# A windowed attention and gated feed-forward kernel: unit 1's attention in the wide band form, a new order of work, three aligned places in TensorE's code

## The chip, the core and the metric

The kernel runs on one core of a Trainium2 chip. The core has TensorE (matrix products), VectorE, ScalarE and GpSimd (elementwise work), SyncE (which issues the DMAs here), an on-chip memory, and eight banks of PSUM into which TensorE writes. The metric is the device time of one execution, in microseconds.

In the profile's rows PE is TensorE's matmuls and PEld its weight loads, DVE is VectorE, ACT ScalarE, POOL GpSimd, SP SyncE.

## The reference

Attention over 8 batches and 8 heads, 576 positions of 64 values, in which a position sees itself and the 63 before it; then a feed-forward stage with token shift and a gate. Everything is float32.

```
scores = (q @ k.T) / sqrt(64)
mask   = (rel >= 0) & (rel < 64)          # rel = pos[:, None] - pos[None, :]
attn   = softmax(where(mask, scores, -1e9))
x      = (attn @ v), heads side by side   # 8 x 576 x 512
xk = mu_k * x + (1 - mu_k) * x_prev       # x_prev: one position back
xr = mu_r * x + (1 - mu_r) * x_prev
k  = relu(xk @ w_k)                       # 512 -> 1024
out = sigmoid(xr @ w_r) * ((k * k) @ w_v)
```

The weights and `v`, `q`, `k` come as the reference gives them; the weights arrive as 64-bit words and are decoded on the chip.

## The kernel before

**Units and groups.** The 8 x 576 positions are cut into nine units of 512 positions. A unit has four groups, one for each pair of heads (128 of the 512 columns), so there are 36 groups `g`; two neighbouring groups make a pair `j = g // 2`. For each unit the attention of its four groups gives `xT`, `mix` turns that into the operands `xs` (or `xm` in unit 0) of the products, and `r_units`, `k_units` and `v_units` do the three products with 512 columns each.

**Three forms of attention.** The first four groups (unit 0, `WHOLES`) work on blocks of 128 x 128 and transpose on TensorE. Groups 4 to 7 (unit 1, below `WIDE`) have four bands of 32 partitions, each with four blocks of 32 queries of one group: per group 32 score calls and 48 value calls. From group 8 on (`g >= WIDE`) a pair of groups shares its bands: two bands a group, each with eight blocks of queries, half of the score work of both groups in each of the two calls, so that a score call needs the queries and keys of both groups; the values need 40 calls a group. A call in float32 stands in the machine's code as two weight loads and two matmuls, so a pair's values are 192 matmuls below `WIDE` and 160 from it on, and its scores 128 in either form. The softmax between them runs as `least` and `exp` (VectorE, ScalarE), `shares` (sums and reciprocals), `scale` (GpSimd or VectorE) and `turn`, VectorE's transposition, one for each group and half (lines 778 to 853).

**The stage before the products.** In unit 0 the weights are decoded: each of 20 parts (4 of `w_r`, 8 of `w_k`, 8 of `w_v`) passes `sign` (ScalarE), `clamp`, `shift`, `top`, `low` (VectorE, some clamps on GpSimd), `first_part` and `second_part` (lines 405 to 455). Unit 0's r and k products use `low`'s output straight, as `whole`, in float32; everything else uses the two halves, `ws`, three matmuls to a product of 128 x 512.

**What sets the order.** Every step is a `Piece` with the engines it may run on, a cost, what it needs and which buffers it takes (`room`: 8 banks, 2 `qk` buffers, 3 `v` buffers, and so on). `play()` lays the pieces out on a modelled clock; `p.fn(p.engine)` then emits them in that order, and each engine runs its instructions in the order emitted. `ORDER` (line 86) fixes by number what each engine plays first, which covers unit 0, unit 1 and the beginning of unit 2; after that `play()` chooses by key and by the modelled clock, in which TensorE's costs come from `clocked`. `Hold` counts the uses of a buffer.

**What the steps below touch.** `values` (line 643) writes the value calls; at the first group of a pair it can call `addr_align` (line 650), which places the next instruction of TensorE's code at a given slot; up to `max_nops` slots are filled with idle instructions, and more are jumped over. With `PLACED = 18` no pair is ever placed, since `j` ends at 17. `load_v` (line 559) loads the value blocks, six of 32 rows to a band and group below `WIDE`, five from it on. `first_mask` (line 368) writes the two masks for bands with a batch's first queries.

Of the kernel before, what the change touches and what calls it, by code (L numbers as in the profile page):

```python
# [33 lines left out]
NC, NF = DM // P, DF // P  # L34
# [15 lines left out]
WHOLE = 859  # L50
# [12 lines left out]
WIDE = 8  # L63
# [14 lines left out]
ALIGN, SKIP = 102, 12  # L78
PLACED = 18
# [5 lines left out]

ORDER = {
# [10 lines left out]
    ),  # L97
    "DVE": (
# [12 lines left out]
    ),  # L111
    "ACT": (
# [11 lines left out]
    ),  # L124
    "POOL": (
# [4 lines left out]
    ),  # L130
# [17 lines left out]
def attn_rwkv_kernel(ctx, tc, qT, kT, v2, mu_k, mu_r, w_k, w_v, w_r, out):  # L148
# [49 lines left out]
    def play():  # L198

        left, free, now, begun, port, bus, landed, run = {}, {}, 0, [], 0, 0, [], None  # L200
        moved, clock = 0, [WINDOW, 0, True]
# [5 lines left out]
        def clocked(t, work):  # L207
            ratio = 2.37 if work == 440 else 1.92
            tick(t)
            while True:  # L210
                r = ratio if clock[2] else 1
                if t + work * r <= clock[0]:
                    clock[1] += work * r
                    return t + work * r
                clock[1] += clock[0] - t
                work, t = work - (clock[0] - t) / r, clock[0]
                tick(t)
# [19 lines left out]
        while any(left.values()) or any(script.values()):  # L237
# [8 lines left out]
            for e, ps in left.items():  # L246
# [3 lines left out]
                for _, n, p in ([(0, 0, given[-1])] if given else ps):  # L250
# [29 lines left out]
                    if e == "PE":  # L280
                        free[e] = p.done = clocked(now, p.costs[e])
                    else:
                        free[e] = p.done = now + p.costs[e]
# [359 lines left out]
    def values(g):  # L643

        j, n = divmod(g, 2)
        if n == 0:
            flipped[j] = [bank(2 * P) if g >= WIDE else bank(2, P) for _ in bands]

            if j >= PLACED:
                tc.keep_in_program_order(nc.tensor.addr_align(128, offset=ALIGN, max_nops=SKIP))  # L650
# [65 lines left out]
    def run_x(keys, j):  # L716
# [35 lines left out]
        for n, g in enumerate(pair):  # L752
            needs = every[n] if whole else sum(every, [])
            uses = [*held["v", g], *(chain.pop((g, h, "pt")) for h in range(2))]
            if whole:
                for half in range(2) if g in HALVES else (None,):
                    one = [Hold("bank"), Hold("x"), Hold("x")]
                    part = 1 if half is None else 2
                    p = Piece("PE", keys[n], 1100 / part, lambda e, g=g, half=half: whole_values(g, half),
# [5 lines left out]
            p = Piece("PE", keys[0], (1091 if ps else 1340) - 170 * (g >= WIDE), lambda e, g=g: values(g), [*needs, *ps], [x for o in own for x in o], uses)  # L765
# [322 lines left out]
    def begin(k):  # L1088
        return BEGIN[k] if k < len(BEGIN) else 10 * k - 60
# [10 lines left out]
    for g in range(PAIRED):  # L1100
        if g >= NC:
            load_qk(g, key=begin(g - 1) - 1)
            load_v(g, key=begin(g) - 1)
        if g == WHOLES:
            built = Piece("POOL", begin(g) - 8, 3300, band_mask, port=True)
            built = chain["masks"] = Piece("POOL", begin(g) - 4, 900, lambda e: first_mask(e, 0), [built, chain["least"]], port=True)
        run_s(begin(g), g, 1000 if g < WHOLES else 870)
        if g < WHOLES:
            for h in range(2):
                turn_whole(begin(g) + 1, g, h)  # L1110
        if g % 2:
            run_x((begin(g - 1) + 2, begin(g) + 2), g // 2)
    for j in range(PAIRED // 2, len(groups) // 2):
# [3 lines left out]
        if 2 * j % NC == 0 and u in (2, 4):  # L1117
            built = chain["masks"] = Piece("POOL", pair_at(j) - 4, 1200, lambda e, b=u // 4: first_mask(e, b, b + 2),
                                           [built, *chain.pop("firsts")], port=True)
        before = None  # L1120
        for g in (2 * j, 2 * j + 1):
            p = run_s(pair_at(j), g, 970 if before else 870)
# [67 lines left out]
```

## Time and profile before

| | us |
|---|---|
| median of three runs (613.45 to 615.07) | 614.35 |
| the profiled execution's own time | 613.81 |
| its span, first to last instruction | 612.0 |
| TensorE busy | 596.7 |
| VectorE busy | 395.0 |
| ScalarE busy | 371.0 |
| GpSimd busy | 141.9 |

All rows come from the one profiled execution, whose span is 1.81 us shorter than its time. TensorE is busy in every fortieth of the span to nine tenths or more but the first and the last. A matmul's row is its start, its length with a modelled end, and how many follow each other on the same tiles; the distance between the starts of two rows is what TensorE spent on the first.

### The profile page before, as it was taken

To read this page: it belongs to the slowest core of one execution; us is meant where nothing else is said; L and a number is where in the kernel's file an instruction comes from. 1 tells how busy PE (TensorE), PEld (TensorE's weight loads), DVE (VectorE), ACT (ScalarE), POOL (GpSimd) and SP (SyncE) were. 2 spreads that over 40 slices of the span, in tenths; PEclk is the share of its full clock that TensorE was granted. 3 is DMA by queue.
4 is the path that set the end of the run, shared out by engine and by line. 5 is a ranking of instruction groups with operands and counts; after the bars stand their busy time and mean duration, and the time that the engine had idled before them with its cause. 6 is when DMAs were issued, how large, how long until landed. Compare 5 with 4: busy or idle time off the path is not lost.

```text
span 612.0 us, 17692 instructions
## 1 busy us (share of the span) xinstructions
PE 596.7 (98%) x7072; PEld 465.6 (76%) x7072; DVE 395.0 (65%) x1208; ACT 371.0 (61%) x1060; POOL 141.9 (23%) x208
## 2 busy tenths in 40 slices
PE   4999999999999999999999999999999999999997
PEld 3654577878888888888888888877888888888885
DVE  4899999909783667556763677276827583665211
ACT  5988967448476736683577358644766466734630
POOL 6575557502300230011201130023002300201000
PEclk9999999999999999999999999999999999999999
DMA  8997122213431223122312222132212230010001
GB/s 252 337 331 224 54 86 81 70 51 83 132 93 43 76 73 116 29 75 71 101 42 59 91 77 74 44 109 80 76 44 93 74 97 24 2 54 17 1 18 52
DMA packets 57426, 53.59 MB, mean 88 GB/s; under 512 B 10496, under 2 KB 50944, under 8 KB 57344
## 3 DMA queue, kind: packets, MB, share of 16 engines
q1 hardware_dynamic: 57344, 52.46, 28.1%
q8 instruction: 56, 0.92, 0.6%
q14 instruction: 26, 0.21, 0.1%
HBM read 43.00 MB, written 9.44 MB: 86 GB/s over the span
## 4 chain that ended last, share of the span: by engine, by line
PE 88%; DMA 7%; ACT 2%; DVE 1%; SPq 1%; issue 1%; ACTq 0%
PE bank L166 88%; DMA raw<-w_v 3%; DMA v<-v 2%; SPq L166 1%; DMA raw<-w_k 1%; DMA qk<-kT 1%; ACT pr L166 1%; DVE bank L166 1%; ACT kf L166 1%; DVE r L166 0%; ACT ws L166 0%; ACT wt L166 0%; DVE rs L166 0%; ACT ks L166 0%; DVE whole L166 0%
## 5 line engine op out<-in xcount | busy, mean ns | idle before, releaser
L166 PE MATMUL bank<-xs,ws 128*128 128x512 f32 x1152 | 273.2, 396 | 0.0
L166 PEld LDWEIGHTS bank<-xs,ws 128*128 128x128 f32 x1152 | 215.8, 188 | 50.9
L166 PE MATMUL bank<-ks,ws 128*128 128x512 f32 x864 | 206.7, 397 | 1.4 <-issue 1.4
L166 PEld LDWEIGHTS bank<-ks,ws 128*128 128x128 f32 x864 | 161.0, 188 | 40.2 <-issue 1.5
L166 DVE TENSOR_TENSOR ks<-kf,ks 128x512 fp32r<-128x512 f32 x69 | 51.1, 746 | 112.9 <-ACT ks L166 112.9
L166 ACT ACTIVATE pr<-pr,nmax 128x96 f32<-128x96 f32 (+1 forms) x288 | 105.0, 366 | 11.7 <-DVE nmax L166 11.1
L166 ACT ACTIVATE kf<-bank 128x512 f32<-128x512 f32 x72 | 43.0, 597 | 67.3 <-PE bank L166 65.4
L166 POOL CAST ks<-kf 128x512 fp32r<-128x512 f32 x8 | 4.9, 611 | 256.0 <-ACT kf L166 256.0
L166 DVE CUSTOM_DVE_ANT_0 pr<-bank,bands 128x96 f32<-128x96 f32 x256 | 49.4, 249 | 13.4 <-PE bank L166 13.2
L166 ACT COPY xT<-bank 128x256 f32<-128x256 f32 (+1 forms) x46 | 15.7, 391 | 65.1 <-PE bank L166 64.9
L166 ACT ACTIVATION_READ_ACCUMULATOR pr<-pr,nmax 128x1 f32 x288 | 54.1, 188 | 0.0
L166 ACT ACTIVATE kf<-kf 128x512 f32<-128x512 f32 x71 | 44.7, 631 | 1.9
L166 DVE SCALAR_TENSOR_TENSOR r<-bank,r 128x512 f32<-128x512 f32 x36 | 24.5, 680 | 32.3 <-PE bank L166 32.3
L166 PE MATMUL bank<-xm,whole 128*128 128x512 f32 x96 | 43.8, 601 | 1.0 <-DVE whole L166 1.0
L166 ACT ACTIVATE th<-bank 128x512 f32<-128x512 f32 x36 | 21.3, 591 | 35.8 <-PE bank L166 24.6
L166 PEld LDWEIGHTS bank<-pt,v 32*64 32x64 f32 (+1 forms) x2720 | 35.7, 131 | 9.4 <-issue 7.1
L166 ACT CAST ks<-kf 128x512 fp32r<-128x512 f32 x64 | 39.5, 619 | 1.7
L166 PE MATMUL bank<-qk 64*32 64x96 f32 (+1 forms) x2112 | 33.4, 254 | 7.3 <-DMA qk<-qT 5.9
L166 PEld LDWEIGHTS bank<-qk 64*32 64x32 f32 (+1 forms) x2112 | 28.2, 108 | 15.3 <-issue 12.5
L166 PE MATMUL bank<-pt,v 32*64 32x96 f32 (+3 forms) x2720 | 38.6, 243 | 0.3 <-ACT kf L166 0.3
L166 DVE TENSOR_TENSOR xs<-d,xs 128x512 fp32r<-128x512 f32 x59 | 37.9, 685 | 0.0
L166 ACT CAST xs<-d 128x512 fp32r<-128x512 f32 x49 | 28.8, 617 | 14.2 <-POOL d L166 12.7
(79 smaller groups left out, 547.4 us busy)
## 6 DMA issues: line engine op xcount, KB each, us to landing
v<-v SPq DMA_DIRECT2D x76, 64.0 KB, 2.1
raw<-w_k SPq DMA_DIRECT2D x8, 512.0 KB, 7.2
raw<-w_v SPq DMA_DIRECT2D x8, 512.0 KB, 5.6
v<-v SPq DMA_DIRECT2D x52, 48.0 KB, 2.0
v<-v SPq DMA_DIRECT2D x68, 32.0 KB, 2.0
raw<-w_r SPq DMA_DIRECT2D x4, 512.0 KB, 6.0
outT<-r SPq DMA_DIRECT2D x8, 256.0 KB, 2.1
qk<-kT SPq DMA_DIRECT2D x8, 224.0 KB, 4.2
```

The costliest lines, as they stand in the source:

```text
L166: return lambda *args, **kw: tc.keep_in_program_order(op(*args, **kw))
```

## The change

`WIDE` goes from 8 to 4, so unit 1's groups 4 to 7 take the form of the later units: `values`, `scores`, `load_v`, `run_s`, `run_x` and `soften` follow by their conditions on `g`. Their queries, keys and values are loaded two groups at a time, and the masks for a batch's first queries are made once for units 1 to 3 (bands 0 and 2) and once more at unit 4, where before they were made for unit 1, for unit 2 and for unit 4.

`addr_align` is now called for pairs 3, 6 and 11, with slots 228, 59 and 56 of 256, before the pair's values.

`play()` has two costs more, `ENTER` and `LEAVE`, when TensorE goes from full to tiled matmuls and back, and other costs for the tiled pieces. The tables in `ORDER` are new and shorter; the rest of the order follows `play()` as before.

```
-WIDE = 8
+WIDE = 4
...
-ALIGN, SKIP = 102, 12
-PLACED = 18
+PLACES, SKIP = {3: 228, 6: 59, 11: 56}, 12
...
+ENTER, LEAVE = 95, 281
...
 ORDER = {
     "PE": (
-        509, 510, 535, 531, 566, 533, 559, 557, 561, 555, 590, 563, 1503, 1510, 1517, 586, 1524, 588, 633, 1518,
+        509, 510, 535, 531, 566, 533, 559, 561, 557, 555, 590, 563, 1502, 1509, 1516, 1523, 588, 586, 645, 614,
...
-        def clocked(t, work):
-            ratio = 2.37 if work == 440 else 1.92
+        def clocked(t, work, ratio):
...
                     if e == "PE":
-                        free[e] = p.done = clocked(now, p.costs[e])
+                        work, at = p.costs[e], now
+                        before, tiled = tiled, work not in (440, 697, WHOLE)
+                        if before is not None and tiled != before:
+                            at = clocked(at, ENTER if tiled else LEAVE, 1)
+                        free[e] = p.done = clocked(at, work, 1.8 if tiled else 2.37 if work == 440 else 1.92)
...
-            if j >= PLACED:
-                tc.keep_in_program_order(nc.tensor.addr_align(128, offset=ALIGN, max_nops=SKIP))
+            if j in PLACES:
+                tc.keep_in_program_order(nc.tensor.addr_align(256, offset=PLACES[j], max_nops=SKIP))
...
-            p = Piece("PE", keys[0], (1091 if ps else 1340) - 170 * (g >= WIDE), lambda e, g=g: values(g), [*needs, *ps], [x for o in own for x in o], uses)
+            p = Piece("PE", keys[0], 908 if g >= WIDE else 1074, lambda e, g=g: values(g), [*needs, *ps], [x for o in own for x in o], uses)
...
-        if g >= NC:
-            load_qk(g, key=begin(g - 1) - 1)
-            load_v(g, key=begin(g) - 1)
+        for x in range(g, g + 2) if g >= WIDE and g % 2 == 0 else [g] if NC <= g < WIDE else []:
+            load_qk(x, key=begin(x - 1) - 1)
+            load_v(x, key=begin(x) - 1)
...
-            built = chain["masks"] = Piece("POOL", begin(g) - 4, 900, lambda e: first_mask(e, 0), [built, chain["least"]], port=True)
-        run_s(begin(g), g, 1000 if g < WHOLES else 870)
+            built = chain["masks"] = Piece("POOL", begin(g) - 4, 900, lambda e: first_mask(e, 0, 2), [built, chain["least"]], port=True)
+        run_s(begin(g), g, 900 if g < WHOLES else 740)
...
-        if 2 * j % NC == 0 and u in (2, 4):
-            built = chain["masks"] = Piece("POOL", pair_at(j) - 4, 1200, lambda e, b=u // 4: first_mask(e, b, b + 2),
+        if 2 * j % NC == 0 and u == 4:
+            built = chain["masks"] = Piece("POOL", pair_at(j) - 4, 1200, lambda e: first_mask(e, 1, 3),
```

Three places show what moves. First TensorE around unit 1's first values; `xm,whole` are unit 0's r and k products, `ks,ws` its v products, `pt,v` values, and a row's count is of calls, each value call being two matmuls. Before:

```order
MATMUL bank<-xm,whole 128x512 x8
MATMUL bank<-pt,v 64x96 x8
MATMUL bank<-pt,v 64x32 x16
MATMUL bank<-pt,v 64x64 x8
MATMUL bank<-pt,v 64x96 x8
MATMUL bank<-pt,v 64x64 x8
MATMUL bank<-ks,ws_961 128x512 x3
MATMUL bank<-ks,ws_1063 128x512 x3
MATMUL bank<-xm,whole 128x512 x2
MATMUL bank<-pt,v 64x96 x8
```

Now, from the same product on:

```order
MATMUL bank<-xm,whole 128x512 x7
MATMUL bank<-ks,ws_940 128x512 x3
MATMUL bank<-xm,whole 128x512 x2
MATMUL bank<-pt,v 64x96 x16
MATMUL bank<-pt,v 64x64 x8
MATMUL bank<-pt,v 64x32 x8
MATMUL bank<-pt,v 64x64 x8
MATMUL bank<-pt,v 64x96 x32
MATMUL bank<-pt,v 64x32 x8
MATMUL bank<-xm,whole 128x512 x2
MATMUL bank<-ks,ws_1048 128x512 x3
```

The first pair's values were two visits of 48 calls, with products between them; they are one visit of 80 calls now.

Second, VectorE's first steps; `ISA pr,nmax<-bank` with the `ISA nmax` behind it is one `least`, `TENSOR_SCALAR wt<-wt` a clamp and `TENSOR_SCALAR bank<-wt` a shift of the first weight part. Before:

```order
ISA pr,nmax<-bank,mask_92 128x128
ISA nmax 128x1
ISA pr,nmax<-bank,mask_92 128x128
ISA nmax 128x1
ISA pr,nmax<-bank,maskNone 128x128
ISA nmax 128x1
TENSOR_SCALAR bank<-wt 128x512
ISA pr,nmax<-bank,maskNone 128x128
```

Now:

```order
TENSOR_SCALAR wt<-wt 128x512
TENSOR_SCALAR bank<-wt 128x512
ISA pr,nmax<-bank,mask_92 128x128
ISA nmax 128x1
ISA pr,nmax<-bank,maskNone 128x128
ISA nmax 128x1
```

The clamp has moved from GpSimd to VectorE, and both steps on the first weight part stand ahead of the first `least`.

Third, TensorE at pair 6, one of the aligned places; `xs,ws` are r and k products of a later unit. Before:

```order
MATMUL bank<-xs,ws_967 128x512 x3
MATMUL bank<-xs,ws_1278 128x512 x3
MATMUL bank<-pt,v 64x96 x16
MATMUL bank<-pt,v 64x64 x8
MATMUL bank<-pt,v 64x32 x8
MATMUL bank<-pt,v 64x64 x8
MATMUL bank<-pt,v 64x96 x32
```

Now:

```order
MATMUL bank<-xs,ws_1150 128x512 x3
MATMUL bank<-xs,ws_904 128x512 x3
ISA
MATMUL bank<-pt,v 64x96 x16
MATMUL bank<-pt,v 64x64 x8
MATMUL bank<-pt,v 64x32 x8
MATMUL bank<-pt,v 64x64 x8
MATMUL bank<-pt,v 64x96 x32
```

The `ISA` row is the alignment, between the last product and the pair's first value call.

## Rows read from the trace of the kernel before

**Rows 1.** The page's busy times: us, share of the span, instructions.

```profile
PE 596.7 (98%) x7072; PEld 465.6 (76%) x7072; DVE 395.0 (65%) x1208; ACT 371.0 (61%) x1060; POOL 141.9 (23%) x208
```

**Rows 2.** The chain of waits in order of time: start us, us, what.

```profile
72.73 341.73 PE bank L166 x3718
414.46 1.36 issue
```

**Rows 3.** Three stretches: length, busy us of each engine, clock, DMA share, GB/s.

```profile
22.00:72.00 50.00, 49.04 (x439) 23.76 (x439) 48.29 (x147) 45.27 (x132) 29.58 (x36) 1.00 0.74 235
86.30:123.00 36.70, 36.70 (x459) 29.49 (x458) 35.80 (x81) 20.39 (x62) 22.60 (x21) 1.00 0.24 71
140.00:612.00 472.00, 467.06 (x5522) 377.93 (x5520) 282.57 (x883) 269.75 (x765) 66.75 (x97) 1.00 0.22 65
```

**Rows 4.** What TensorE's matmuls waited for: us in total, times, longest us.

```profile
PE bank L166 <- DVE whole L166: 1.0, 2, 0.7
```

**Rows 5.** TensorE's timeline, 86 to 98 us: start, us, engine, instruction, count.

```profile
86.26 2.40 PE L166 MATMUL bank<-pt,v 32*64 32x96 f32 x192
88.59 5.14 PE L166 MATMUL bank<-ks,ws 128*128 128x512 f32 x21
93.67 1.00 PE L166 MATMUL bank<-qk 64*32 64x96 f32 x64
94.60 1.66 PE L166 MATMUL bank<-ks,ws 128*128 128x512 f32 x6
96.19 0.99 PE L166 MATMUL bank<-qk 64*32 64x96 f32 x64
97.11 5.15 PE L166 MATMUL bank<-ks,ws 128*128 128x512 f32 x21
```

**Rows 6.** TensorE's timeline at the end of the span.

```profile
552.50 33.63 PE L166 MATMUL bank<-xs,ws 128*128 128x512 f32 x144
585.97 22.45 PE L166 MATMUL bank<-ks,ws 128*128 128x512 f32 x96
```

**Rows 7.** TensorE's timeline, visits of unit 2 and the runs behind them.

```profile
123.11 1.17 PE L166 MATMUL bank<-pt,v 32*64 32x96 f32 x80
124.21 5.84 PE L166 MATMUL bank<-xs,ws 128*128 128x512 f32 x24
...
140.36 1.73 PE L166 MATMUL bank<-qk 64*32 64x96 f32 x128
142.02 14.27 PE L166 MATMUL bank<-ks,ws 128*128 128x512 f32 x60
```

**Rows 8.** VectorE's timeline: the last two transpositions for the value visit at 86.26.

```profile
85.05 1.03 DVE L166 STREAM_TRANSPOSE pt<-pr 128x384 f32<-128x384 f32 x2
```

**Rows 9.** VectorE's timeline, two waits of the first stage, in brackets with their releaser.

```profile
8.60 0.69 DVE L166 TENSOR_SCALAR bank<-wt 128x512 uint32<-128x512 uint32 x1 [0.87 <-POOL wt L166]
...
21.01 0.75 DVE L166 SCALAR_TENSOR_TENSOR xm<-xT,mur,xm 128x512 f32<-128x512 f32 x1 [0.74 <-POOL xm L166]
```

**Rows 10.** GpSimd's timeline: the first clamp and the first scaling.

```profile
7.95 0.61 POOL L166 TENSOR_SCALAR wt<-wt 128x512 f32<-128x512 f32 x1
12.19 1.04 POOL L166 TENSOR_TENSOR pr<-pr,rs 128x512 f32<-128x512 f32 x1 [3.62 <-DVE rs L166]
```

**Rows 11.** VectorE's timeline: the second half of the last `w_v` part.

```profile
96.94 0.69 DVE L166 TENSOR_TENSOR ws<-wt,ws 128x512 fp32r<-128x512 f32 x1
```

**Rows 12.** TensorE's timeline: the value visit ahead of the gap.

```profile
412.40 2.06 PE L166 MATMUL bank<-pt,v 32*64 32x96 f32 x160
```

**Rows 13.** The page's DMA queue for TensorE's code: packets, MB, share.

```profile
q8 instruction: 56, 0.92, 0.6%
```

**Rows 14.** DMA traffic, 412 to 416 us, in 40 slices of 0.1 us.

```profile
GB/s 200 31 0 0 0 0 0 0 0 0 0 0 0 0 164 0 0 0 0 0 0 0 0 0 0 0 0 0 0 10 51 169 118 123 21 46 144 41 92 5
```

**Rows 15.** TensorE's timeline: two value visits without a gap behind them.

```profile
252.09 2.06 PE L166 MATMUL bank<-pt,v 32*64 32x96 f32 x160
284.07 2.06 PE L166 MATMUL bank<-pt,v 32*64 32x96 f32 x160
```

More of the change, by code (lines that the diff above doesn't have):

```diff
@@ L200, in play @@
         left, free, now, begun, port, bus, landed, run = {}, {}, 0, [], 0, 0, [], None
-        moved, clock = 0, [WINDOW, 0, True]
+        moved, clock, tiled = 0, [WINDOW, 0, True], None
         def tick(t):
@@ L758, in run_x @@
                     part = 1 if half is None else 2
-                    p = Piece("PE", keys[n], 1100 / part, lambda e, g=g, half=half: whole_values(g, half),
+                    p = Piece("PE", keys[n], 900 / part, lambda e, g=g, half=half: whole_values(g, half),
                               needs if half is None else [*arrived["v", g], needs[half - 2]], one, uses)
@@ L1121, in attn_rwkv_kernel @@
         for g in (2 * j, 2 * j + 1):
-            p = run_s(pair_at(j), g, 970 if before else 870)
+            p = run_s(pair_at(j), g, 740)
             if before:
```

80 rows, old and new, of the table ORDER are left out of this document.

## The prediction

> **What bounds the kernel now.** I read the page first: TensorE is busy for 596.7 of 612.0 us [rows 1], so the time is TensorE's list of work plus the little that it waits. The chain of waits says where that is: from 72.73 us on it is TensorE alone, but for a gap of 1.36 us at 414.46 that nothing in the profile released ("issue") [rows 2]. So there are two stages. Before 72.7 us VectorE shares the bound: it is busy 48.29 of the 50 us from 22 to 72, and 35.80 of the 36.7 us from 86.3 to 123 [rows 3], with decoding the weights, the softmax and the first products' operands. TensorE waits for it twice, 1.0 us together, for a decoded weight [rows 4]. After 140 us VectorE has slack, 282.57 of 472 [rows 3], and only TensorE's own list counts.
>
> **The price list of TensorE**, from start to start in its timeline. A long unbroken run takes 33.47 us (552.50 to 585.97) for 144 matmuls of 512 columns, 0.2324 each [rows 6]. The 21 between two groups of small tiled matmuls last 5.08 (88.59 to 93.67) [rows 5], 0.20 more than 21 x 0.2324 = 4.88: that is one entry into the tiled groups and one exit. A value visit in the form of unit 1 takes 2.33 for 192 matmuls, a score visit of 64 takes 0.93 and 0.92 [rows 5]; 80 values in the wide form take 1.10, a score visit of 128 takes 1.66 [rows 7]. A whole pair's 160 values take 1.99: the 2.06 that their rows give [rows 15] less the 0.07 by which each such row's end (its last matmul's) overlaps the next start, as at 86.26 (2.40 against 2.33).
>
> **The change, part by part.**
>
> (1) *Unit 1 in the wide form.* Each of its two pairs of groups needs 160 value matmuls instead of 192, and both groups' queries and keys before its first score. 0.26 MB fewer values are loaded (16 blocks of 16 KB); no wait of TensorE names a value load, so that is priced at nothing. The new order also joins what stood in pieces: the first pair of unit 2 has one score visit instead of two and one value visit instead of two.
>
> I do not credit this at its face, because VectorE gates the place. In the old order the value visit of 192 began at 86.26, and VectorE's last two transpositions for it ended at 86.08 [rows 5, 8]; in the new order the second pair's values also need all four transpositions of their pair. I counted VectorE's steps up to the last of them in both orders: 168 and 168, of the same kinds but for one scaling of 384 columns fewer and one copy of 512 more, by their pitch 0.47 less and 0.60 more. So VectorE owes 0.13 us more at that gate. TensorE itself would be there sooner: ahead of it now stand the same matmuls of the first unit, 3 fewer `ks` matmuls, 32 fewer values and fewer visits. So the gate binds, and the sum starts at it.
>
> From that gate on, old: 2.33 + 0.93 + 0.92 + 1.10 + 1.10 + five visits x 0.20 = 7.38. New: values 1.99, scores 1.66, values 1.99, three visits x 0.20 = 6.24. Less 1.14; but three `ks` matmuls that stood ahead of the gate now stand behind it, 3 x 0.23 = 0.70. Net **-0.44**.
>
> (2) *When VectorE reaches the gate.* Old: it stood 0.87 us until 8.60 for GpSimd's clamp, which ran from 7.95, and 0.74 us for GpSimd's `xm` before its first blend at 21.01 [rows 9, 10], with 11.55 us of work behind it by then. New: the clamp is its own first step, so it starts near 7.95 and has 12.0 us queued ahead of that blend, without the 0.87; the first reciprocals stand ahead of two decode steps, so GpSimd's first scaling, which waited 3.62 us until 12.19 [rows 10], can start about 1 us sooner, and the 0.74 shrinks. 7.95 + 12.0 = 19.95 against 21.01. Carried whole to the gate that is 21.01 - 11.55 - 7.95 = 1.5 us of lost time less 0.13 more of work, -1.4; carried not at all, 0; a loss is possible too, since the fourth part of `w_r` now comes behind 1.5 MB more of loads: +1, as long as TensorE's waits for decoded weights were [rows 4]. I take **-1.0**, nearer the full value because VectorE has under 2 us of idle time between 22 and 72 in which it could vanish.
>
> (3) *The last weight part.* VectorE made the second half of the last `w_v` part at 96.94 [rows 11], the second score visit ended at 97.11 [rows 5], and the first matmul that uses that half stood three matmuls later, at 97.8: just in time. In the new order this step stands 3.9 us of work later on VectorE, and TensorE asks for it 15 matmuls into its third `ks` run, near 100.6. With VectorE 1.4 us ahead that is a wait of 0 to 0.9; I take **+0.4**.
>
> (4) *The three aligned places.* After the value visit at 412.40 [rows 12] TensorE stands the 1.36 us. Queue 8 carries code, 56 packets of 16 KB (0.92 MB) [rows 13], for 14,144 matmuls and weight loads: some 253 in a packet. One of them moved at 413.4 [rows 14], 2.4 us before the work went on at 415.82. A value visit is 320 instructions in 1.99 us, 6 ns each, so it runs through a packet of code in 1.6 us, where the 512-column runs take 30: only a visit that swallows a whole packet can outrun the next one. Taking 256 instructions to a block, as the changed code does, and a block's start at the gap, the visit at 412.40 began at slot 188. By the same count those at 252.09 and 284.07 began at slots 172 and 226, and they took the usual 2.06 [rows 15]. Counting the new list from its aligned places (228, 59, 56), its visits start at slots 19 to 131, 166, 169, 221, 223 and 229: none between 172 and 219. So the gap goes, **-1.36**; the two that stand 3 and 5 slots nearer than 226 could cost 8 x 0.116 = 0.9 in all, at one slot of a 512-column run each. For the padding itself I take nothing, since nothing executes in it, and bound it among the rivals.
>
> A page speaks against this term. The Trainium skill, "Runtime: NRT & Kernel Launch", section "Instruction fetch mechanics", says that crossing a 16 KiB boundary is mostly hidden, because instructions are dispatched slower than they are refilled. By that the term would be 0 and the forecast 1.4 us longer; the gap of 1.36 us, behind a visit of small tiles, does not bear it out.
>
> **Sum.** -0.44 - 1.0 + 0.4 - 1.36 = -2.4 us. The profiled execution took 613.81 (span 612.0 and 1.81 around it), so 611.4; the median of the three runs, 614.35, lies 0.54 above that execution, so the forecast is **611.9**.
>
> **The rivals.**
>
> *VectorE comes no sooner* (its early gain is lost in other waits, or the wider loads cost it): 1.0 over the forecast, 612.9, and 613.9 if it comes 1 us later than before. For it: with VectorE at 97% and ScalarE at 91% of that stage [rows 3] a local gain is easily lost. Against: the 0.87 us is plain idle time.
>
> *TensorE isn't gated.* The joined visits and the 1.0 us of waits for decoded weights count in full, some 1.2 us more, and the wait of (3) goes: 610.3. For it: the old transpositions may only have been as early as they were needed. Against: the 168 steps ahead of them.
>
> *The alignment does not reach its slots*, or another visit meets the same fate: 1.4 over, 613.3.
>
> *Slower: the padding throws the fetched code away.* At two of the places the padding is, by my count, 127 and 237 instructions, over the 12 that the code allows as idle ones, so the engine must jump over it. If the jump drops the block that was fetched ahead, TensorE stands for a fetch each time, 2.4 us by the packet of 413.4, twice: 616.7. It decides against the change once both fetches lie bare; where the matmuls queued ahead, 0.23 each, cover them, it costs nothing. No row of the old kernel shows a jump. The same section of that page says that a taken branch forces a fetch where its target lies outside the window held; here the target lies in the next block.
>
> **Chances.** Forecast 0.48; VectorE no sooner 0.22; not gated 0.11; alignment missed 0.11; jumps 0.08. A measurement tells 0.3% (1.84 us): faster is under 612.5, slower over 616.2. Of the forecast's own spread of about 1 us 0.7 lies under 612.5: 0.34, with 0.11 (not gated), 0.08 of VectorE's case and 0.03 of the alignment's: 0.56. Slower 0.08, same 0.36. The range: low 609.6 (not gated, nothing lost in (3) and VectorE's gain whole), high 614.4 (VectorE 1 us late and 0.5 of a stall).
>
> **What would show it.** Right: no "issue" wait over 0.5 us on TensorE after 100 us; three value visits of 160 by 130 us, near 2.0 each; the second pair's values begin between 84.5 and 86, right behind a transposition; VectorE's first blend near 20. Wrong: those values begin after 86.3; a wait of over 1 us in the `ks` runs for a weight part; a gap of 1 to 3 us at an aligned place.

## The result, and the profile after

The changed kernel takes 617.85 us (median of ten runs, 617.06 to 621.57), the kernel before 614.5 in the same comparison: a ratio of 1.0071, interval 1.0054 to 1.0088. It is 3.4 us slower, where the forecast was 2.4 us faster, and the time lies outside the range. The profiled execution took 617.70 us; its span is 615.8 against 612.0.

First the chain of waits of the changed kernel from 44 us on (start us, us, what); it answers to [rows 2]:

```profile
44.77 39.84 PE bank L163 x425
84.61 2.17 issue
86.78 199.16 PE bank L163 x2056
285.94 1.56 issue
287.50 160.63 PE bank L163 x1716
448.13 1.83 issue
449.96 162.29 PE bank L163 x1310
```

Before, the chain from 72.73 us on held one stretch in which TensorE waited for nothing that the profile shows ("issue"); now there are three. TensorE's busy time is the same to 0.5 us (597.2 against 596.7 in [rows 1]), so they are what the reader has to look at. TensorE's timeline around each of the three (start, us, instruction, count, idle before it):

```profile
82.69 1.92 PE L163 MATMUL bank<-pt,v 32*64 32x96 f32 x140
86.78 0.47 PE L163 MATMUL bank<-pt,v 32*64 32x96 f32 x20 [2.17 <-issue]
87.18 9.48 PE L163 MATMUL bank<-ks,ws 128*128 128x512 f32 x33
96.59 0.67 PE L163 MATMUL bank<-qk 64*32 64x96 f32 x35
...
283.99 1.95 PE L163 MATMUL bank<-pt,v 32*64 32x96 f32 x144
287.50 0.35 PE L163 MATMUL bank<-pt,v 32*64 32x32 f32 x16 [1.56 <-issue]
287.78 8.63 PE L163 MATMUL bank<-ks,ws 128*128 128x512 f32 x36
...
446.18 1.95 PE L163 MATMUL bank<-pt,v 32*64 32x96 f32 x145
449.96 0.34 PE L163 MATMUL bank<-pt,v 32*64 32x32 f32 x15 [1.83 <-issue]
450.24 15.82 PE L163 MATMUL bank<-xs,ws 128*128 128x512 f32 x60
465.99 1.25 PE L163 MATMUL bank<-qk 64*32 64x96 f32 x88
```

Each gap lies inside a value visit, after 140, 144 and 145 of its 160 matmuls. From start to start the three visits last 4.49, 3.79 and 4.06 us where the others last 1.99: 2.50, 1.80 and 2.07 lost. The 33 products behind the first take 9.41 us (87.18 to 96.59) instead of 33 x 0.2324 + 0.20 = 7.87, the 60 behind the third 15.75 (450.24 to 465.99) instead of 14.14: 1.54 and 1.61 more. The clock says why; columns as in [rows 3], the clock is the third figure from the end:

```profile
88.20:90.50 2.30, 2.30 (x7) 1.80 (x6) 2.27 (x5) 0.00 (x0) 0.33 (x1) 0.56 0.36 101
450.40:451.80 1.40, 1.40 (x4) 1.12 (x5) 0.98 (x2) 0.82 (x3) 0.00 (x0) 0.50 0.37 90
287.60:290.00 2.40, 2.40 (x26) 1.96 (x27) 2.06 (x5) 1.87 (x4) 0.00 (x0) 1.00 0.34 92
```

Soon after the first and the third gap TensorE runs at half its clock (0.5, 1.2 GHz) for some eight products, 0.427 us each (the first row also holds a little time at the full clock); behind the second it does not.

So the changed kernel loses 2.50 + 1.54 + 1.80 + 2.07 + 1.61 = 9.5 us at three places, and the old gap (3.42 from 412.40 to 415.82, less 1.99 = 1.43) is gone. Net 8.1 lost, and the span grew by 3.8 only: some 4.3 us were gained elsewhere. Where, the row of unit 2's second score visit shows, which began at 140.36 in [rows 7]:

```profile
140.40 1.73 PE L163 MATMUL bank<-qk 64*32 64x96 f32 x128
```

Up to here both have done the same stages, and the changed kernel comes 0.04 us later although it lost 4.04 us at its first gap. In these two executions the gain of 4.0 us lies ahead of 140 us.

### The profile page after: what moved, and what is told of

Read it like the earlier page. It is cut to its first block, busy times and chain, and to the rows that moved or that the text cites. A ratio compares the mean times of both kernels' runs of the same rounds, so it can differ in the third digit from the quotient of the medians.

```text
span 615.8 us, 17548 instructions
## 1 busy us (share of the span) xinstructions
PE 597.2 (97%) x7008; PEld 467.3 (76%) x7008; DVE 393.6 (64%) x1210; ACT 370.7 (60%) x1057; POOL 141.0 (23%) x205
## 4 chain that ended last, share of the span: by engine, by line
PE 93%; DVE 4%; issue 1%; DMA 1%; POOL 0%; SPq 0%; ACT 0%; ACTq 0%; POOLq 0%
PE bank L163 93%; DVE bank L163 1%; DVE xm L163 1%; DMA qk<-qT 1%; DVE whole L163 1%; DVE pr L163 1%; SPq L163 0%; POOL pr L163 0%; DVE rs L163 0%; DVE r L163 0%; DVE wt L163 0%; POOL wt L163 0%; ACT wt L163 0%; ACT pt L163 0%; DVE pt L163 0%
## 5 line engine op out<-in xcount | busy, mean ns | idle before, releaser
L163 DVE COPY xT<-bank 128x256 f32<-128x256 f32 x26 | 10.4, 421 | 47.9 <-PE bank L163 47.9
```

The source lines that it names most:

```text
L163: return lambda *args, **kw: tc.keep_in_program_order(op(*args, **kw))
```

## The experiments

The theory: a value visit's place in TensorE's code decides. A block of code is 256 instructions, a value visit of 160 matmuls is 320 in 2 us; one that crosses two borders of blocks has to wait for the second block if that block's fetch begins only when the first border is crossed. The rivals: the aligned place itself stops TensorE, or the transfers of that moment do. Slots are counted as in the prediction.

**Three places moved, or taken out.** e1_clear sets the changed kernel's places so that no visit begins in the band that loses, e2_plain takes them out:

```
-PLACES, SKIP = {3: 228, 6: 59, 11: 56}, 12
+PLACES, SKIP = {3: 9, 6: 64, 11: 62}, 12      # e1_clear
+PLACES, SKIP = {}, 12                         # e2_plain
```

> The changed kernel with its three places moved: slots 9, 64 and 62 instead of 228, 59 and 56. Counted from them, the sixteen value visits begin at slots 87, 10, 137, 168, 65, 119, 174, 228, 27, 63, 118, 172, 227, 25, 78 and 132 of a block of 256 instructions. Theory (position): a value visit of 320 instructions loses 1.3 to 2.4 us when it begins so that it crosses two block borders and the first of them lies over 30 instructions into it, that is at slots from about 180 to 225; the three gaps of the changed kernel, 2.4, 1.8 and 2.1 us, and the two stretches at the lower clock behind two of them, 1.55 each, all go: 617.85 less 9.4 = 608.4, and TensorE has no issue wait over 0.5 us behind 70 us. Rival (the aligned place itself stops TensorE, by the jump over its padding or by the instruction that marks it): the gap at the first place stays and new ones come at the others, 613 to 618. Second rival (the transfers of that moment make the fetch late, whatever the slot): gaps of about 2 us stay near 285 and 447 us, 613 to 616.

> The changed kernel with no aligned place at all. By count its visits then begin at 87, 229, 100, 131, 189, 243, 42, 96, 151, 205, 4, 58, 113, 167, 220 and 18. Theory (position): gaps of 1.3 to 2.1 us behind the visits at 189 (near 185 us), 205 (near 345) and 220 (near 510), none at 285 and 447; 1.5 us more behind each gap of 2 us or more, where the clock falls. The first unit's second visit still begins at 229, with nothing between it and the products, so its gap of 2.4 us shows whether the slot or the marking instruction made it: stays by the slot, goes by the instruction. In all 614 to 619. Rival (the aligned place stops TensorE): no gap anywhere, 608.4.

e1_clear took 610.63 us, a ratio of 0.9936 (0.9918 to 0.9953): 4.3 us faster than the kernel before in its comparison (614.94), and 7.2 under the changed kernel's 617.85. No gap is left; TensorE's waits of over 0.5 us are these, all ahead of 100 us (who was waited for, us, times, longest):

```profile
PE bank L163 <- DMA qk<-kT: 5.5, 1, 5.5
PE bank L163 <- DVE whole L163: 2.2, 1, 2.2
PE bank L163 <- DMA qk<-qT: 1.8, 1, 1.8
PE bank L163 <- DVE wt L163: 0.9, 1, 0.9
PE bank L163 <- DVE xm L163: 0.8, 1, 0.8
```

e2_plain took 622.29 (1.0113, 1.0084 to 1.0142). Its four gaps lie at the four visits named, slots 229, 189, 205 and 220; three of them:

```profile
86.75 0.47 PE L163 MATMUL bank<-pt,v 32*64 32x96 f32 x21 [1.57 <-issue]
191.87 0.18 PE L163 MATMUL bank<-pt,v 32*64 32x32 f32 x1 [1.65 <-issue]
517.92 0.38 PE L163 MATMUL bank<-pt,v 32*64 32x96 f32 x17 [2.00 <-issue]
```

Both rivals fall: the gaps come without any aligned place, at other moments than before, and e1_clear jumps three times over padding (37, 95 and 238 instructions by count) without a gap. One remainder is open: at slot 229 e2_plain loses 1.88 us from start to start and the changed kernel, with the place ahead of it, 2.50; a jump may have a part in those 0.6 us (see the slower rival below). e2_plain is slower than expected because all four gaps came, 7.7 us in all from start to start, and the clock fell behind three of them. e1_clear is 2.2 us over its expectation. In its profile 0.9 is a longer wait for a decoded weight near 45 us, 2.18 ("DVE whole") against 1.32 in the changed kernel's execution; e2_plain, e5_waits, e6_clamp_back and e8_low_first show 2.2 as well, so the 1.32 was the exception. For the rest the gaps had hidden something, below.

**The old kernel, its gap taken away and given more.** The edit is one table in place of `PLACED`:

```
-            if j >= PLACED:
-                tc.keep_in_program_order(nc.tensor.addr_align(128, offset=ALIGN, max_nops=SKIP))
+            if j in PLACES:      # {13: 11} in e3_before_moved, {6: 199} in e4_before_hit
+                tc.keep_in_program_order(nc.tensor.addr_align(256, offset=PLACES[j], max_nops=SKIP))
```

> The kernel before with one aligned place, slot 11, ahead of the values of pair 13, whose visit at 412 us began at slot 188 and stood for 1.36 us; five visits begin now at slots 12, 67, 121, 174 and 228. Theory (position): the gap goes and none comes, 1.36 us less than before, 613.1, ratio 0.998. Rival (the jump over the 80 instructions of padding costs a fetch): 1 to 2.4 us of gap at the place, 614.5 to 616.

> The kernel before with one aligned place, slot 199, ahead of the values of pair 6, so that the visits behind it begin at 200, 0, 55, 109, 164, 218, 17, 71, 126, 180, 233 and 31. Theory (position): two gaps appear in a kernel that had none there, 1.7 to 2.1 us at the visits near 188 (slot 200) and 348 us (slot 218), 0 to 0.8 at the visit near 476 (slot 180), and the old one at 412 goes; with 1.5 us at the lower clock behind each gap of 2 us or more: 616.5 to 620. Rival (the gaps belong to the changed order, not to the slot): only the old gap goes, 613.1.

e4_before_hit took 621.95 (1.0124, 1.0103 to 1.0145): the old order gets the same gaps where a visit is put into the band. It has them at slots 200 and 218 as expected, 0.37 us at slot 180 (in the products behind the visit), and one that was not expected, at slot 233, which lost 2.5 us, with the clock at half behind it, and puts the time over the expected 620:

```profile
191.21 0.31 PE L166 MATMUL bank<-pt,v 32*64 32x32 f32 x6 [2.01 <-issue]
353.33 0.34 PE L166 MATMUL bank<-pt,v 32*64 32x32 f32 x14 [1.84 <-issue]
485.46 1.78 PE L166 MATMUL bank<-ks,ws 128*128 128x512 f32 x7 [0.37 <-issue]
517.93 0.75 PE L166 MATMUL bank<-pt,v 32*64 32x96 f32 x22 [1.93 <-issue]
```

e3_before_moved took 614.56 (1.0002, 0.9987 to 1.0017). The gap at 414 us went (the visit starts at 412.58 and the products behind it at 414.57), but the last visit, moved to slot 228, lost 1.96 us where the gap at 414 us had cost 1.43, against the expectation that 228 was safe:

```profile
544.35 0.47 PE L166 MATMUL bank<-pt,v 32*64 32x96 f32 x19 [1.64 <-issue]
```

**What sets the upper edge.** Visits at slots 226, 227 and 228 of pairs 9 and 14 had lost nothing. In the listed code a visit's first calls carry waits, and some waits stand as instructions of their own. One opens every visit; the first behind it stands 32 instructions into the visits of pairs 9 and 14, 24 into pair 17's, 16 into those of pairs 16 and 3. e5_waits puts the visits of pairs 9, 14, 16 and 17 at slot 236 (and pair 3's at 245):

```
-PLACES, SKIP = {3: 228, 6: 59, 11: 56}, 12
+PLACES, SKIP = {3: 244, 6: 64, 9: 235, 11: 62, 14: 235, 16: 235, 17: 235}, 12
```

> The changed kernel with seven aligned places, so that the value visits of pairs 9, 14, 16 and 17 all begin at slot 236 of a block (pair 3 at 245, the others outside the band that loses). Open so far: visits that began at 226, 227 and 228 (pairs 9 and 14) lost nothing, others that began at 228 (pair 17), 229 (pair 3) and 233 (pair 16) lost 1.8 to 2.2 us. Theory (first wait): TensorE's instructions are read ahead into a visit as far as the first instruction in it that does nothing but wait for a semaphore; in the listed code that stands 32 instructions into the visits of pairs 9 and 14, 24 into that of pair 17, 16 into those of pairs 16 and 3. A border that lies ahead of it is crossed early and its fetch starts before the visit, one behind it is not. With the border 20 instructions in, pair 16 (near 504 us) alone loses 1.7 to 2.2 us, the fetches of pairs 9, 14 and 17 start 1 to 3 us before their visits: 610.6 + 1.8 = 612.4, or 613.9 with a stretch at the lower clock. Rival (a fixed slot is the edge, for every visit): either all four lose, 617 to 623, or none, 610.6.

Measured 615.60 (1.0007, 0.9994 to 1.0021). Of the four, pair 16 alone has a gap; pair 9's, 14's and 17's visits last their 1.99 us. The visits of pairs 9, 16 and 17, with what follows each:

```profile
282.70 2.06 PE L163 MATMUL bank<-pt,v 32*64 32x96 f32 x160
284.69 3.52 PE L163 MATMUL bank<-ks,ws 128*128 128x512 f32 x14
...
507.30 1.85 PE L163 MATMUL bank<-pt,v 32*64 32x96 f32 x136
510.85 0.51 PE L163 MATMUL bank<-pt,v 32*64 32x96 f32 x24 [1.71 <-issue]
...
542.78 2.06 PE L163 MATMUL bank<-pt,v 32*64 32x96 f32 x160
544.77 3.52 PE L163 MATMUL bank<-ks,ws 128*128 128x512 f32 x14
```

The DMA traffic shows the fetches. In the 3.2 us ahead of pair 9's visit queue 8 moves one packet of code (first row); in the 3.3 us ahead of pair 16's nothing moves at all (second row), and its packet comes in the 1.7 us behind the visit's start, in the 29th of 40 slices, 1.2 us into it (third and fourth):

```profile
q8 instruction: 1, 0.02, 2.5%
...
DMA packets 0, 0.00 MB, mean 0 GB/s; under 512 B 0, under 2 KB 0, under 8 KB 0
...
GB/s 0 0 0 0 0 0 0 0 0 0 0 0 0 0 0 0 0 0 0 0 0 0 0 0 0 0 0 0 386 0 0 0 0 0 0 0 0 0 0 0
...
q8 instruction: 1, 0.02, 4.0%
```

So one fixed slot is not the edge. What fits is the visit's first inner instruction that only waits: with the border ahead of it the next block is asked for 1 to 3 us before the visit, with the border behind it 1.0 to 1.7 us after the visit's start. That accounts for the unexpected slots 228 (pair 17, edge 232) and 233 (pair 16, edge 240), and for the changed kernel's 223 and 221 (pairs 9 and 14, edge 224), one and three slots short. That this wait is the cause is not shown: no run moves such a wait by itself, and the trace records pair 16's wait as passed 2.39 us ahead of the visit, while the packet came 1.2 us behind its start. And one miss is left: pair 3 began at 245, behind its edge of 240, and lost 2.0 us all the same (82.56 to 86.53). With that the expected 613.9, which has the lower clock behind pair 16's gap in it, becomes 615.9, near the measured time. Pair 3's values wait for VectorE's last transposition, which ended 0.56 us before the visit, where the other visits have theirs 3.9 us and more ahead; the read-ahead may have stood at that wait, but no run separates it. Pairs 3 and 16 also lie behind jumps (16 and 149 instructions by count), but so does pair 17 (202), which lost nothing.

**VectorE's start.** Two runs move the clamp of the first weight part (piece 6) and its shift (piece 7), in the tables of `ORDER`:

```
# e6_clamp_back, from e1_clear            # e7_clamp_alone, from the kernel before
 DVE  -6, 7, 511, 513, 517, 521,           DVE  -511, 515, 517, 7, 521,
      +511, 513, 517, 7, 521,                   +6, 7, 511, 515, 517, 521,
 POOL -643, 520,                           POOL -631, 6, 520,
      +643, 6, 520,                             +631, 520,
```

> The changed kernel with the three places at 9, 64 and 62 (610.63 in the last comparison), and the clamp of the first weight part given back to GpSimd, with the shift behind it where the kernel before had it. Theory: VectorE came to unit 1's second pair 3.95 us sooner than before because these two steps, 1.1 us, moved into time in which it had nothing to do, 5.06 to 6.70 us, and the rest followed; back on GpSimd, the shift waits until GpSimd's clamp ends near 8.7. VectorE's last transposition for that pair and the second half of the first score visit of unit 2, which waits for VectorE, come 0.7 to 1.2 us later: 611.3 to 611.8. Rival (the gain came from the order of VectorE's later steps): less than 0.3 us later, 610.6.

> The kernel before with that one step alone: the clamp of the first weight part and the shift behind it as VectorE's first two steps. Theory: VectorE's wait of 0.87 us until 8.60 goes and its work of 1.1 us moves ahead of 6.7 us; the value visit that began at 86.26 right behind a transposition begins 0.8 to 1.5 us sooner, and the time is as much less: 613.1 to 613.8 against 614.6. Rival (the gain is taken up again by the order behind it): no difference over 0.3 us, 614.6.

e7_clamp_alone took 613.33 (0.9976, 0.9964 to 0.9989), 1.5 us less (0.7 to 2.2): in the old order the two steps alone do that. The times show it, not the profile: its visit behind the gate starts at 85.42 against 86.26 in [rows 5], but e4_before_hit, which has the old code up to there, starts it at 85.31. VectorE's first step is at 5.11:

```profile
5.11 0.43 DVE L166 TENSOR_SCALAR wt<-wt 128x512 f32<-128x512 f32 x1 [5.11 <-ACT wt L166]
...
85.42 2.40 PE L166 MATMUL bank<-pt,v 32*64 32x96 f32 x192
```

e6_clamp_back took 611.02 (0.9936, 0.9922 to 0.9950), 0.4 us over e1_clear by the medians and the same by the ratios. In its profile the second score visit of unit 2 starts at 139.44 against 138.40, but that is not the clamp: this execution, the slowest of its six, ran at half clock behind the wait near 45 us, and the 18 products there took 9.62 us (to 55.18) where e1_clear's took 7.92 (to 53.55). First e6_clamp_back, then e1_clear:

```profile
45.56 9.69 PE L163 MATMUL bank<-xm,whole 128*128 128x512 f32 x18 [2.17 <-DVE whole L163]
...
45.63 7.99 PE L163 MATMUL bank<-xm,whole 128*128 128x512 f32 x18 [2.18 <-DVE whole L163]
```

The 1.70 lost there is more than the 1.04 by which the visit is late. So in the new order the step is not shown to be worth anything; up to some 1 us can't be excluded. That is the expectation's rival.

**What the gaps had hidden.** In e1_clear TensorE waits next in unit 2's first score visit, for a bank that VectorE frees with the last step of the last weight part's decode. e8_low_first moves that step (piece 178) up:

```
-        169, 170, 176, 767, 1640, 177, 1645, 84, 1650, 178, 772, 1655,
+        169, 170, 176, 767, 1640, 177, 178, 1645, 84, 1650, 772, 1655,
```

> The changed kernel with the three places at 9, 64 and 62, and on VectorE one step moved: the step that ends the decode of the last weight part (and frees the bank that the second half of unit 2's first score visit waits for) stands ahead of two blends and a half of a weight part instead of behind them. Theory: with the three gaps gone, TensorE's next wait is this one, 1.13 us at 94.14 (0.60 and 0.65 in the two other profiles that have it); it goes, and nothing takes its place before 100 us: 610.63 - 0.6 to 1.1 = 609.5 to 610.0. Rival (VectorE is late as a whole there, so that the xs products behind it wait instead): 610.6, with a new wait of 0.5 to 1 us between 96 and 104 us.

It took 609.97 (0.9919, 0.9902 to 0.9937), the lowest of all, but not apart from e1_clear by its interval. The wait, here in e1_clear's timeline of TensorE, went:

```profile
93.37 1.01 PE L163 MATMUL bank<-qk 64*32 64x96 f32 x66
95.27 0.97 PE L163 MATMUL bank<-qk 64*32 64x96 f32 x62 [0.89 <-DVE wt L163]
```

But the rival came true in part. In e8_low_first another wait appears 4 us later, for a weight part, 17 products into the third run on `ks`:

```profile
93.05 1.75 PE L163 MATMUL bank<-qk 64*32 64x96 f32 x128
94.73 4.22 PE L163 MATMUL bank<-ks,ws 128*128 128x512 f32 x17
99.62 2.59 PE L163 MATMUL bank<-ks,ws 128*128 128x512 f32 x10 [0.67 <-DVE ws L163]
```

**What the wide form and the order are worth.** e9_before_both is the kernel before with the clamp as in e7_clamp_alone and places {13: 11, 17: 99}.

> The kernel before with two things alone: the clamp of the first weight part and its shift as VectorE's first steps (-1.5 us by its own run), and two aligned places, slots 11 and 99 ahead of the values of pairs 13 and 17, so that no visit begins in the band that loses (-1.36, the gap at 414 us). Narrow form and order as before. Theory: the two add up, 614.9 - 1.5 - 1.36 = 612.0, and what the changed kernel without its gaps (610.63) is better by, 1.4 us, is the wide form and the order. Rival (wide form and order are worth nothing once VectorE starts early): 610.6.

It took 611.34 (0.9943, 0.9925 to 0.9961), without a gap. e1_clear's 0.9936 is 0.4 us better, well inside both intervals: the wide form and the new order together are not shown to be worth anything beyond the clamp and the gaps; 1.4 us, as expected, is not excluded either (by the medians, each against its own comparison, it is 1.3).

## Why the prediction was wrong, point by point

**(4) failed, and decided the sign.** The old gap was explained rightly: code, one block late, behind a visit that swallows a whole block; e3_before_moved and e4_before_hit show it. What failed is the step "none between 172 and 219; the two that stand 3 and 5 slots nearer than 226 could cost 0.9 in all". It took the one visit without a gap at 226 [rows 15] for a point on a slope of 0.116 us a slot. The upper edge is a step: at 226 the fetch starts 1.5 us before the visit, at 223 and 221 1.1 us behind its start, so that most of it lies bare. The visit's first inner wait fits as the edge, with the open points above. The visits at 223 and 221 cost 1.80 and 2.07 + 1.61 us instead of 0.9. The visit at 229 was held safe by the same row; it belongs to another pair and cost 2.50 + 1.54. At the lower edge such a slope does fit the two visits there are: 0.37 us at 180 and 1.36 at 188 [rows 2], 0.124 a slot. The term came out at +8.1 instead of -1.36: 9.5 of new losses less the 1.43.

The Trainium skill, "Runtime: NRT & Kernel Launch", section "Instruction fetch mechanics", holds the crossing of a 16 KiB boundary for mostly hidden, since instructions are dispatched slower than they are refilled. The measurement decides: it is hidden in the runs of 512 columns, and not where a run of 6 ns an instruction crosses two borders with the first fetch not asked for early; there it cost 1.4 to 2.5 us a time (e4_before_hit's slot 180 less).

**The rival that "another visit meets the same fate" was the right one, and mis-sized.** It had 0.11 and 613.3, together with the case that the alignment doesn't reach its slots. The places did reach them (the gaps come 280 to 290 instructions into visits counted at 221 to 229, so at 509 to 511, the second border); that the fate would meet three visits at once and take the clock with it was not in its price.

**The slower rival had the wrong mechanism.** Padding that throws code away was to give 616.7, near the measured 617.85, but no gap stands at a jump: the one behind the changed kernel's first place begins 280 instructions into the visit, and comes again in e2_plain without the place. That first place is a jump too, though the prediction counted two: the aligning instruction takes a slot itself, so by count the next slot 228 lies 255 further on. A packet of code moves 3.2 us ahead of this visit, as at e1_clear's three jumps, and none does in e2_plain; the changed kernel moved 57 packets, e2_plain 55.

**(2) was a quarter of what came, and its premise "So the gate binds" was wrong.** TensorE stands at the gate in neither kernel. Before, the 33 products ahead of the visit took 7.86 us (78.40 to 86.26), by the price list 33 x 0.2324 + 0.20 = 7.87; the values were ready 0.18 us ahead, and 0.57 ahead in the changed kernel (82.12 and 82.69). What moved is TensorE's own list: its first product on `xm` starts 2.13 us sooner, and from there to the gate it takes 62.71 us instead of 64.15. Before (two rows), then after:

```profile
22.11 2.84 PE L166 MATMUL bank<-xm,whole 128*128 128x512 f32 x6
78.40 7.93 PE L166 MATMUL bank<-ks,ws 128*128 128x512 f32 x33
...
19.98 3.70 PE L163 MATMUL bank<-xm,whole 128*128 128x512 f32 x8
```

The rival "TensorE isn't gated" (0.11, 610.3) had that right; without the gaps the change takes 610.63 (e1_clear), nearer to it than to 611.9, though not for all of its reasons.

VectorE had to come sooner too, and did. Its last transposition for the second pair ended at 82.12 (81.10 + 1.02) instead of 86.08 [rows 8], 3.96 us sooner, not 1.0:

```profile
5.06 0.43 DVE L163 TENSOR_SCALAR wt<-wt 128x512 f32<-128x512 f32 x1 [5.06 <-ACT wt L163]
...
81.10 1.02 DVE L163 STREAM_TRANSPOSE pt<-pr 128x384 f32<-128x384 f32 x2
```

"It starts near 7.95" failed as well. That was when GpSimd got to the clamp [rows 10], after its masks; its input came from ScalarE and was there at 5.06. VectorE's list, 168 steps in both, so begins 1.94 us sooner (5.06 against the first `least` at 7.00), its waits of over 0.1 us on the way to the gate shrank from 3.96 to 2.71 us in all, and its steps ran 0.8 us faster; the blend forecast at 20 came at 18.89. But the early start is not the larger part. e6_clamp_back gives it back (first step at 6.75) and still ends its last transposition at 83.94, in spite of the 1.70 us at half clock; e7_clamp_alone, the early start in the old order, ends it at 85.22. The rest belongs to the order of the other steps, and no run takes that apart. Nor is 3.96 the typical gain: with the same code up to the gate the visit starts at 86.26, 86.39 and 85.31 in the three profiles of the old order and between 82.56 and 83.51 in the five of the new one, 2.9 us sooner on average.

**(1) held as a count of TensorE's work; that its stretch came out right was luck.** From the start of the second pair's values to 140.4 us the forecast was -0.44. The start moved from 86.26 to 82.69, 3.57 sooner; at 140.4 the lead is 4.0 with the first gap's 4.04 put back, so the stretch itself is 0.4 us shorter. But the gap had covered a wait. Without it, in e1_clear, the stretch takes 54.89 us (83.51 to 138.40) against 54.10 before; 1.13 of them are the wait for the bank, which no term of the prediction has, and without that wait it would be 53.76, 0.3 us shorter. e9_before_both says that of this gain little may be left in the whole.

**(3) was right, and hidden.** No wait for the last weight part shows in the changed kernel, since TensorE had lost 4 us just before and VectorE was ahead. In e8_low_first, with gaps and bank wait gone, it is there, 0.67 us idle against +0.4 with bounds of 0 and 0.9. That is also why taking 9.5 us of losses out gave 7.2 back: part of the first gap stood where TensorE would have waited for VectorE, 1.13 us from matmul to matmul in e1_clear's score visit, and e1_clear's profile comes to the gate 0.82 us later (83.51 against 82.69).

## What to carry to other kernels

Count where tight runs of small matmuls begin in the engine's code, and measure it again after every change that adds or drops instructions: here the place of a 2 us run within 256 instructions was worth more than the change of form itself. Of the starts seen, those at slots 0 to 174 lost nothing; from there the second border lies 18 instructions, nine long products, or more behind the run's end. At 180 and above some lost, and the upper end was not the same for every visit, so keep away from it. And when one stall goes or comes, look for the wait that it had covered: the sum of the stalls is not what their removal returns.

## What the hardware showed that was not expected

How early the next block of TensorE's code is asked for went with the place of an instruction that only waits for a semaphore: of four visits at the same slot, 236, only the one whose first inner wait stands ahead of the border lost 2.0 us. Pair 3's visit at 245 is the exception. The jumps over padding cost nothing visible: eight of them, over 16 to 238 instructions, in e1_clear and e5_waits, all without a gap at the place (only the 0.6 us at the changed kernel's first place may be a jump's); the two gaps in visits behind them, those of pairs 3 and 16 in e5_waits, begin 264 and 272 instructions into the visit, at the second border, and e2_plain has gaps in both pairs' visits without a jump. And the clock fell to half for some eight products behind some gaps and not behind others, not by their length: behind 1.57 us of idle time (86.75 in e2_plain) it fell, behind 2.01 (191.21 in e4_before_hit) it did not. What decides is not shown by any run here.
